# Moving TensorE transposes to DMA from tile 6 on, with two load buffers, later scores and split last rows, in a local attention + squared-ReLU kernel

## Chip, cores, metric

One core of one Trainium2 chip. The time is the device time of one execution in microseconds (us), the median of several. The page and the views of the profile are from one profiled execution each. A profiled span is about 1.8 us shorter than the time of the same run (before: span 220.5, time 222.32).

## The reference

```python
# attention: B, H, S, D = 4, 8, 768, 64; 8 global keys, 96 local ones
scores = q @ k.T / sqrt(D) + bias            # bias = -slope(head) * distance
scores = where(keep, scores, -1e9)           # keep: global or within the 96 before
a = softmax(scores);  x = a @ v              # x: 3072 tokens x 512
# two layers: w_in 512 x 2048, w_out 2048 x 512
h = x @ w_in;  r = maximum(h, 0);  out = (r * r) @ w_out
```

## The kernel before

The tokens are 24 tiles of 128 (six to a batch), and two tiles make a block of the two layers. For each tile: load q, k, v (cast to bf16 on the way, issued by GpSimd), transpose q and k, scores `sc`, exp on ScalarE, bias, `po` = weights @ v, normalise to `x`, transpose x. For each block, in eight steps: `hT` (first layer, 8 matmuls of 256 columns), relu on ScalarE, square on VectorE, `acc` (second layer, two pairs of 512 columns). A small planner in Python fixes each engine's order at build time, from guessed durations. TensorE runs that order strictly, so one operand that is late holds up all that stands behind it.

```python
NFIRST = 4; NBIAS = 3
JQK, JX = 10, 10            # from this tile on, q/k and x are transposed by DMA
NQ, NKT = 10, 2 * TPB       # load buffers for q and k
LEADS = {}                  # scores stand 12 steps before the block needs them
qk_ring = [const([P, 2, d_model], BF16, f"qk_{i}") for i in range(NQ)]
...
# below JQK: four transposes on TensorE into PSUM, one eviction; for q and for k
nc.tensor.transpose(out=tr[:, pair, :], in_=src[:, pair * P:(pair + 1) * P], identity=ident)
any_copy(e, T_[:, n], tr)
# from JQK on: one DMA for both, issued by SyncE
nc.sync.dma_start_transpose(out=T_.rearrange("p n a c -> p (n a) c"),
                            in_=qk_ring[j % NQ].rearrange("p n c -> p (n c)"))
...
# scores; for the first three tiles a second matmul adds the bias
nc.tensor.matmul(out=sc[odd, g][:, at, :], lhsT=..., rhs=..., start=True, stop=j >= NBIAS)
nc.tensor.matmul(out=sc[odd, g][:, at, :], lhsT=sid[2 * pair + odd], rhs=pb, start=False, stop=True)
...
# last block: first 128 rows over all steps, then the other 128 (whole width);
# the last rows leave PSUM as two halves of one bank: ScalarE, then VectorE; two stores
```

The softmax here doesn't subtract the row's maximum and nothing guards it: scores larger than these inputs give would overflow.

Of the kernel before, what the change touches and what calls it, by code (L numbers as in the profile page):

```python
# [11 lines left out]
FP32 = mybir.dt.float32  # L12
BF16 = mybir.dt.bfloat16
# [8 lines left out]
class Plan:  # L22
# [6 lines left out]



    LAG = {"PE": 0.25, "ACT": 0.15, "DVE": 0.12, "SP": 2.6, "POOLQ": 2.5, "DMA": 0.0}
    URGE = 0.05

    def __init__(self):
# [64 lines left out]
def kernel(  # L100
# [11 lines left out]
    nc = tc.nc  # L112
    B, H, S, D = q.shape
    P = 128
# [20 lines left out]
    NFIRST = 4  # L135
    NSPLIT = 4
    NBIAS = 3
    JQK, JX = 10, 10
    NQ, NKT = 10, 2 * TPB
    NG = 8 - NACC  # L140
    G = ("g", NG)

# [6 lines left out]
    def const(shape, dt, name):  # L149
        return consts.tile(shape, dt, name=name, tag=name)  # L150

    qk_ring = [const([P, 2, d_model], BF16, f"qk_{i}") for i in range(NQ)]
    v_sb = [const([P, H, D + 1], BF16, f"v_{j}") for j in range(NT)]

    qkT = [const([P, 2, NPAIR, P], BF16, f"qkT_{i}") for i in range(NKT)]
# [12 lines left out]
    pbt = const([P, 2, P], FP32, "pbt")  # L168
    pbw = const([P, 2, P], FP32, "pbw")
    plan = Plan()  # L170
    LEADS = {}
    NHS = 14
    E_AT = 14.0
    NWARM = 8
# [6 lines left out]
    def landed(name, at):  # L181
        land[name] = plan.op(("land",) + name, {"DMA": 0.0}, None, ready=at)

    def src_rows(x, j):
        b, t = divmod(j, TPB)
        return x[b, :, t * P : (t + 1) * P, :]

    def swdge(name, dst, src, t):
        nc.gpsimd.dma_start(out=dst, in_=src)  # L189
        issue[1] = max(issue[1], issue[0] + 3.3) + t  # L190
        issue[0] += 0.75 if name[0][0] == "w" else 0.88
        land[name] = issue[1] + 0.3

    plain = {}
    for j in range(NPLAIN):
# [12 lines left out]

    def load_part(n, j):
        swdge(  # L210
            ("qk"[n], j), qk_ring[j % NQ][:, n, :].rearrange("p (h d) -> p h d", h=H),
            src_rows((q, k)[n], j).rearrange("h p d -> p h d"), 0.85,
        )

# [117 lines left out]

    tiles = {}
    kT_users = [[] for _ in range(NKT)]
    qk_users = [[] for _ in range(NQ)]
    xT_op = {}
    xT_of = {}
    last_T = [None]
# [2 lines left out]
    for j in range(NT):  # L341
# [6 lines left out]
        if j in late:  # L348
            def emit_load(e, j=j):
                load_tile(j)  # L350
            ld = plan.op(
                ("load", j), {"POOLQ": 2.6}, emit_load, deps=qk_users[j % NQ] + [ones[j]],
                key=base, ready=issue[0],
            )
            qk_users[j % NQ] = []
            land["q", j] = land["k", j] = land["v", j] = ld


# [4 lines left out]
        for n in range(2) if j < JQK else ():  # L363
            users = []

            def emit_tr(e, j=j, n=n, fp=fp):
                tr = ps_g.tile([P, NPAIR, P], FP32 if fp else BF16, name="tr", tag="g")
                src = plain[n, j] if fp else qk_ring[j % NQ][:, n, :]
                for pair in range(NPAIR):
                    nc.tensor.transpose(  # L370
                        out=tr[:, pair, :], in_=src[:, pair * P : (pair + 1) * P],
                        identity=ident32 if fp else ident,
                    )
                tiles["tr", n, j] = tr

            tr = plan.op(
                ("tr", n, j), {"PE": 0.5 if fp else 0.24}, emit_tr,
                deps=[land["qk"[n], j]], key=base, takes=(*G, [users]),
            )

            def emit_T(e, j=j, n=n, T_=T_):
                any_copy(e, T_[:, n], tiles.pop(("tr", n, j)))

            c = plan.op(
                ("T", n, j), {"DVE": 0.7 if fp else 0.43, "ACT": 0.57}, emit_T,
                deps=[tr] + ku, key=base + 0.1,
            )
            users += [tr, c]
            parts.append(c)
            if not fp:  # L390
                qk_users[j % NQ].append(tr)
        if j >= JQK:
            def emit_dT(e, j=j, T_=T_):
                nc.sync.dma_start_transpose(
                    out=T_.rearrange("p n a c -> p (n a) c"),
                    in_=qk_ring[j % NQ].rearrange("p n c -> p (n c)"),
                )

            T = plan.op(
                ("T", j), {"SP": 2.0}, emit_dT,  # L400
                deps=[land["q", j], land["k", j], xT_op[j - 3]] + ku, key=base - 6,
            )
            qk_users[j % NQ].append(T)
            parts = [T]
        kT_users[j % NKT] = ku = []

# [6 lines left out]
        def emit_sc(e, gs, j=j, first=first):  # L413
# [8 lines left out]
                for kt in range(1 if first else 2)  # L422
            ]
            todo = [x for x in todo if x[0] in gs]
            for g, pair, at, kt in todo:
                for odd in range(2):
                    half = slice(odd * D, (odd + 1) * D)
                    nc.tensor.matmul(  # L428
                        out=sc[odd, g][:, at, :],
                        lhsT=qkT[(j - kt) % NKT][half, 1, pair, :],  # L430
                        rhs=qkT[j % NKT][half, 0, pair, :],
                        start=True,
                        stop=j >= NBIAS,
                        skip_group_check=True,
                    )
            for g, pair, at, kt in todo if j < NBIAS else ():
                for odd in range(2):
                    nc.tensor.matmul(
                        out=sc[odd, g][:, at, :],
                        lhsT=sid[2 * pair + odd],  # L440
                        rhs=pb0 if first else pb[:, kt, :],
                        start=False,
                        stop=True,
                        skip_group_check=True,
                    )
# [253 lines left out]

    for blk in range(NBLK):  # L700
        last = blk == NBLK - 1
        acc_users = [[], []]
        order2 = (
            [(s, sub) for sub in range(2) for s in range(NSTEP)]
            if last
            else [(s, sub) for s in range(NSTEP) for sub in range(2)]
        )
        for s, sub in order2:
            users = acc_users[sub]

            def emit_s2(e, blk=blk, s=s, sub=sub):
                if s == 0:
                    tiles["acc", blk, sub] = ps_acc.tile([P, d_model], FP32, name="acc", tag="acc")
                hs = tiles["hs", blk, s]
                for c in range(2):
                    nc.tensor.matmul(  # L716
                        out=tiles["acc", blk, sub],
                        lhsT=hs[:, c, sub * P : (sub + 1) * P],
                        rhs=w_out_sb[s][:, c, :],
                        start=(s == 0 and c == 0),  # L720
                        stop=(s == NSTEP - 1 and c == 1),
                        skip_group_check=True,
# [1 line left out]

            d, husers = square[blk, s]
            o = plan.op(
                ("s2", blk, s, sub), {"PE": 0.43}, emit_s2,
                deps=[d, land["wout", s]] + users[-1:],
                key=8 * blk + s + 2.0 + (50 if last and sub else 0),
                takes=("acc", NACC, [users]) if s == 0 else None,  # L730
            )
            users.append(o)
            husers.append(o)
            if s == NSTEP - 1:

                for half in (0, 1) if last and sub == 1 else (None,):
                    cols = (
                        slice(None)
                        if half is None
                        else slice(half * d_model // 2, (half + 1) * d_model // 2)  # L740
                    )
                    ousers = []

                    def emit_o(e, blk=blk, sub=sub, half=half, cols=cols):
                        o_sb = work.tile([P, d_model], FP32, name="o", tag="o", bufs=4)
                        any_copy(e, o_sb[:, cols], tiles["acc", blk, sub][:, cols])
                        tiles["o", blk, sub, half] = o_sb

                    costs = {"ACT": 0.57, "DVE": 0.62}
                    if half is not None:  # L750
                        costs = [{"ACT": 0.4}, {"DVE": 0.35}][half]
                    ev = plan.op(
                        ("o", blk, sub), costs, emit_o, deps=[o], key=8 * blk + s + 1.0,
                        takes=("o", 4, [ousers]),
                    )
                    users.append(ev)
                    ousers.append(ev)

                    def emit_st(e, blk=blk, sub=sub, half=half, cols=cols):
                        r0 = (blk * 2 + sub) * P  # L760
                        nc.sync.dma_start(
                            out=out[r0 : r0 + P, cols],
                            in_=tiles.pop(("o", blk, sub, half))[:, cols],
                        )

                    st = plan.op(
                        ("st", blk, sub), {"SP": 0.4}, emit_st, deps=[ev],
                        key=8 * blk + s + 9.0,
                    )
                    ousers.append(st)  # L770

    for o in plan.run({"PE": 4.2, "DVE": 4.4, "ACT": 4.2}):
        if o["emit"]:
            o["emit"](o["engine"])

# [34 lines left out]
```

## Time and profile before

221.8 us (221.15 to 222.0, 3 runs). The table is made from the busy times of each engine in stretches of the profiled run (us). "Idle" is the length less TensorE's busy time.

| stretch | length | TensorE idle | what it is |
|---|---|---|---|
| 0 to 12 | 12 | 3.5 | start-up |
| 12 to 30 | 18 | 2.7 | all DMA engines full, weights and first tiles arrive; granted clock 0.50 from 14.1 to 17.5 |
| 30 to 60 | 30 | 1.4 | 1.1 of it is one wait of tile 6 |
| 60 to 200 | 140 | 1.3 | TensorE full: the view of waits has no row here, and 32 of the 2024 matmuls have no record in this trace (1992 records, 2024 of weight loads), so much of the 1.3 need not be idle |
| 200 to 220.5 | 20.5 | 4.7 | last block, 4.1 after the last matmul |

How to read the views: PE is TensorE, PEld its weight loads, DVE VectorE, ACT ScalarE, POOL GpSimd, SP SyncE (SPq: its DMA issues). Rows of digits on a page are the span in 40 equal slices: busy tenths of PE and of the 16 DMA engines (9 is 90% or more), and as PEclk the TensorE clock that was granted, in tenths of full speed. Waits are "who waited <- for whom: us in total, times, longest". The chain by time is "start, us, what". A timeline row is "start, us, engine, line, operation, out<-in, count [idle before <- releaser]". Line numbers shift with the change: scores L428 -> L435, q/k transposes L370 -> L376, first layer L652 -> L661, second layer L716 -> L731, DMA transposes of q and k L394 -> L400, of x L628 -> L637, stores L761 -> L766.

### The profile page before, as it was taken

The numbers are of one execution on the slowest core, as the hardware profiler recorded it, in microseconds if no ns is written. First come the engines' busy times: TensorE is split into PE (matmuls) and PEld (weight loads), VectorE is DVE, ScalarE is ACT, GpSimd is POOL, SyncE is SP. The second block draws the span as 40 slices with busy tenths as digits, with TensorE's granted clock in tenths as the row PEclk, the third lists the DMA queues.
The fourth block names the chain that finished last, engine by engine and source line by source line (L and its number), as shares of the span: only waits on it lengthen the run. The fifth ranks groups of instructions, "written<-read, shape, count | busy, mean of one in ns | idle before, by whom it ended". The sixth has DMA issues, their size and how long they took to land.

```text
span 220.5 us, 5058 instructions
## 1 busy us (share of the span) xinstructions
PE 206.9 (94%) x1992; PEld 143.5 (65%) x2024; DVE 144.0 (65%) x372; ACT 122.5 (56%) x224; POOL 73.7 (33%) x91
## 2 busy tenths in 40 slices
PE   7779879799999999999999999999999999999992
PEld 3658658457667676676667667666667766766740
DVE  5456858647677786775668668666767768745520
ACT  3648865626846657545636736733845744724430
POOL 7997658797962996404000000000000000000000
PEclk9979999999999999999999999999999999999998
DMA  9999999999999999999542532531730620310211
GB/s 129 148 167 200 180 190 192 165 208 161 165 189 131 155 199 145 158 197 132 140 60 48 144 54 45 147 64 33 168 72 4 166 27 12 109 24 16 82 38 59
DMA packets 107304, 26.03 MB, mean 118 GB/s; under 512 B 97936, under 2 KB 104336, under 8 KB 107280
## 3 DMA queue, kind: packets, MB, share of 16 engines
q0 software_dynamic: 79200, 13.37, 82.3%
q1 hardware_dynamic: 28080, 12.33, 25.7%
q8 instruction: 16, 0.26, 0.5%
q14 instruction: 8, 0.07, 0.1%
HBM read 27.26 MB, written 6.29 MB: 152 GB/s over the span
## 4 chain that ended last, share of the span: by engine, by line
PE 77%; DMA 12%; POOL 6%; issue 2%; DVE 1%; ACT 0%; POOLq 0%
PE hT L652 34%; PE acc L716 34%; DMA wout<-in_moe_w_out_dram 4%; PE sc L428 4%; DMA win<-in_moe_w_in_dram 4%; PE po L541 4%; DMA qk<-in_q_dram 4%; POOL qk L189 2%; POOL v L189 2%; POOL win L189 1%; PE tr L370 1%; POOL wout L189 1%; PE trx L604 1%; DVE hs L685 0%; ACT hr L673 0%
## 5 line engine op out<-in xcount | busy, mean ns | idle before, releaser
L652 PE MATMUL hT<-xT,win 128*128 128x256 bf16 x768 | 99.0, 273 | 0.2
L716 PE MATMUL acc<-wout,hs 128*128 128x512 bf16 x352 | 91.5, 379 | 2.0 <-DVE hs L685 0.6
L673 ACT ACTIVATE hr<-hT 128x512 f32<-128x512 f32 x96 | 57.3, 597 | 55.6 <-PE hT L652 54.1
L652 PEld LDWEIGHTS <-win 128*128 128x128 bf16 x768 | 71.1, 98 | 16.7
L685 DVE TENSOR_TENSOR hs<-hr 128x512 bf16<-128x512 f32 x96 | 65.0, 689 | 23.3 <-ACT hr L673 22.5
L716 PEld LDWEIGHTS <-hs 128*128 128x128 bf16 x384 | 36.6, 98 | 29.1 <-DVE hs L685 1.2
L474 ACT ACTIVATE esc<-sc 128x512 bf16<-128x512 f32 x78 | 42.3, 599 | 14.7 <-PE sc L428 14.7
L499 DVE TENSOR_TENSOR at<-esc,E 128x512 bf16<-128x512 bf16 x78 | 32.7, 421 | 8.6 <-ACT esc L474 7.2
L189 POOL DMA_DIRECT2D qk<-in_q_dram x23 | 20.8, 904 | 14.8 <-DMA qkT<-qk 9.0
L189 POOL DMA_DIRECT2D v<-in_v_dram x24 | 21.5, 896 | 7.6 <-DVE at L499 2.7
L189 POOL DMA_DIRECT2D qk<-in_k_dram x23 | 20.6, 897 | 2.8 <-DMA v<-in_v_dram 2.1
L569 DVE TENSOR_TENSOR x<-po,rs 128x256 bf16<-128x256 f32 x48 | 20.4, 424 | 1.7
L541 PEld LDWEIGHTS <-at 128*128 128x128 bf16 x352 | 16.7, 98 | 4.8
L541 PE MATMUL po<-v,at 128*128 128x65 bf16 x352 | 18.5, 193 | 0.0
L428 PEld LDWEIGHTS <-qkT 64*128 64x128 bf16 x352 | 10.0, 95 | 10.9 <-issue 8.0
L568 DVE RECIPROCAL rs<-po 128x4 f32<-128x4 f32 x48 | 8.5, 178 | 10.9 <-PE po L541 10.8
L428 PE MATMUL sc<-qkT 64*128 64x128 bf16 x192 | 13.4, 221 | 1.7 <-ACT qkT L300 0.9
L300 ACT COPY o<-acc 128x512 f32<-128x512 f32 (+1 forms) x15 | 8.4, 573 | 9.2 <-PE acc L716 8.3
L302 DVE COPY o<-acc 128x512 f32<-128x512 f32 (+1 forms) x10 | 6.6, 664 | 9.6 <-PE acc L716 5.0
L428 PE MATMUL sc<-qkT,qkT 64*128 64x128 bf16 x160 | 11.6, 218 | 0.0
L370 PE MATMUL tr<-ident,qk 128*128 128x128 bf16 x72 | 6.8, 225 | 4.0 <-DMA qk<-in_q_dram 2.1
L370 PEld LDWEIGHTS <-qk 128*128 128x128 bf16 x72 | 4.9, 101 | 6.1 <-DMA qk<-in_q_dram 3.0
(40 smaller groups left out, 72.9 us busy)
## 6 DMA issues: line engine op xcount, KB each, us to landing
out_dram<-o SPq DMA_DIRECT2D x23, 256.0 KB, 2.7
v<-in_v_dram POOLq DMA_DIRECT2D x24, 128.0 KB, 7.6
qk<-in_q_dram POOLq DMA_DIRECT2D x23, 128.0 KB, 7.4
qk<-in_k_dram POOLq DMA_DIRECT2D x23, 128.0 KB, 7.7
win<-in_moe_w_in_dram POOLq DMA_DIRECT2D x8, 256.0 KB, 8.1
wout<-in_moe_w_out_dram POOLq DMA_DIRECT2D x8, 256.0 KB, 8.8
plain<-in_q_dram SPq DMA_DIRECT2D x1, 256.0 KB, 3.2
plain<-in_k_dram SPq DMA_DIRECT2D x1, 256.0 KB, 3.9
```

The lines of the kernel that those rows point to most:

```text
L189: nc.gpsimd.dma_start(out=dst, in_=src)
L370: nc.tensor.transpose(out=tr[:, pair, :], in_=src[:, pair * P : (pair + 1) * P], identity=ident32 if fp else ident,)
L428: nc.tensor.matmul(out=sc[odd, g][:, at, :], lhsT=qkT[(j - kt) % NKT][half, 1, pair, :], rhs=qkT[j % NKT][half, 0, pair, :], start=True, s ...
L474: nc.scalar.activation(out=esc, in_=tiles.pop(("sc", j, odd, g)).rearrange("p a c -> p (a c)"), func=Act.Exp, scale=scale,)
L499: nc.vector.tensor_mul(at, tiles.pop(("esc", j, odd, g)), bias)
L541: nc.tensor.matmul(out=po[:, hi, :], lhsT=tiles["at", j, odd, g][:, at * P : (at + 1) * P], rhs=v_sb[kj][:, h, :], start=(i == 0), stop=(i ...
L568: nc.vector.reciprocal(rs, po[:, :, D : D + 1])
L569: nc.vector.tensor_tensor(out=x[:, 4 * hf : 4 * hf + 4, :], in0=po[:, :, :D], in1=rs.to_broadcast([P, 4, D]), op=Alu.mult,)
L652: nc.tensor.matmul(out=hT[:, c, :], lhsT=w_in_sb[s][:, kt, c * P : (c + 1) * P], rhs=tiles["xT", blk][:, kt, :], start=(kt == 0), stop=(kt ...
L673: nc.scalar.activation(hr, tiles.pop(("hT", blk, s)), Act.Relu)
L685: nc.vector.tensor_mul(hs, hr, hr)
L716: nc.tensor.matmul(out=tiles["acc", blk, sub], lhsT=hs[:, c, sub * P : (sub + 1) * P], rhs=w_out_sb[s][:, c, :], start=(s == 0 and c == 0) ...
```

## The change

The intent: take tiles 6 to 9 off TensorE, which bounds the kernel; give those DMA transposes time (scores of tiles 6 and 7 two steps later); replace ten load buffers by six single-use ones and a ring of two; correct the planner's guesses of when data land; split the last 128 rows of the output into column halves, each with its own sum; and set the start flag only on the first score matmul in a PSUM bank, so that the bias adds on to the scores.

```diff
-    LAG = {... "SP": 2.6, "POOLQ": 2.5, "DMA": 0.0}
+    LAG = {... "SP": 2.6, "POOLQ": 0.8, "DMAQ": 1.2, "DMA": 0.0}
-    JQK, JX = 10, 10
-    NQ, NKT = 10, 2 * TPB
+    JQK, JX = 6, 6
+    NQ, NKT = 2, 2 * TPB
-    qk_ring = [... for i in range(NQ)]
+    qk_ring = [... for i in range(NFIRST + 2 + NQ)]
-    LEADS = {}
+    LEADS = {6: 10, 7: 10}
+    def slot(j):
+        return j if j < NFIRST + 2 else NFIRST + 2 + j % NQ
-        land[name] = issue[1] + 0.3
+        land[name] = issue[1] + 0.3 + min(max(0.1 * (issue[1] - 8), 0.0), 1.6)
+            ld = plan.op(("data", j), {"DMAQ": 2.7}, None, deps=[ld], key=base)
 (scores)
-                        start=True,
+                        start=j >= NBIAS or (odd, g) not in opened,
 (last block)
+        parts = [(0, None), (1, 0), (1, 1)] if last else [(0, None), (1, None)]
+            own = half == 1                  # second half: a bank of the other pool
-                        rhs=w_out_sb[s][:, c, :],
+                        rhs=w_out_sb[s][:, c, cols],
-                        costs = [{"ACT": 0.4}, {"DVE": 0.35}][half]
+                    {"ACT": 0.57, "DVE": 0.62} if half is None else {"ACT": 0.37},
 (the rest: index qk_ring by slot(j), and bookkeeping of the planner)
```

More of the change, by code (lines that the diff above doesn't have):

```diff
@@ L22 @@
 class Plan:
-    LAG = {"PE": 0.25, "ACT": 0.15, "DVE": 0.12, "SP": 2.6, "POOLQ": 2.5, "DMA": 0.0}
+    LAG = {"PE": 0.25, "ACT": 0.15, "DVE": 0.12, "SP": 2.6, "POOLQ": 0.8, "DMAQ": 1.2, "DMA": 0.0}
     URGE = 0.05
@@ L150, in const @@
         return consts.tile(shape, dt, name=name, tag=name)
-    qk_ring = [const([P, 2, d_model], BF16, f"qk_{i}") for i in range(NQ)]
+    qk_ring = [const([P, 2, d_model], BF16, f"qk_{i}") for i in range(NFIRST + 2 + NQ)]
     v_sb = [const([P, H, D + 1], BF16, f"v_{j}") for j in range(NT)]
@@ L210, in load_part @@
         swdge(
-            ("qk"[n], j), qk_ring[j % NQ][:, n, :].rearrange("p (h d) -> p h d", h=H),
+            ("qk"[n], j), qk_ring[slot(j)][:, n, :].rearrange("p (h d) -> p h d", h=H),
             src_rows((q, k)[n], j).rearrange("h p d -> p h d"), 0.85,
@@ L334 @@
     kT_users = [[] for _ in range(NKT)]
-    qk_users = [[] for _ in range(NQ)]
+    qk_users = [[] for _ in qk_ring]
     xT_op = {}
@@ L351 @@
             ld = plan.op(
-                ("load", j), {"POOLQ": 2.6}, emit_load, deps=qk_users[j % NQ] + [ones[j]],
+                ("load", j), {"POOLQ": 2.6}, emit_load, deps=qk_users[slot(j)] + [ones[j]],
                 key=base, ready=issue[0],
             )
-            qk_users[j % NQ] = []
+            qk_users[slot(j)] = []
+            ld = plan.op(("data", j), {"DMAQ": 2.7}, None, deps=[ld], key=base)
             land["q", j] = land["k", j] = land["v", j] = ld
@@ L367, in emit_tr @@
                 tr = ps_g.tile([P, NPAIR, P], FP32 if fp else BF16, name="tr", tag="g")
-                src = plain[n, j] if fp else qk_ring[j % NQ][:, n, :]
+                src = plain[n, j] if fp else qk_ring[slot(j)][:, n, :]
                 for pair in range(NPAIR):
@@ L390 @@
             if not fp:
-                qk_users[j % NQ].append(tr)
+                qk_users[slot(j)].append(tr)
         if j >= JQK:
@@ L395, in emit_dT @@
                     out=T_.rearrange("p n a c -> p (n a) c"),
-                    in_=qk_ring[j % NQ].rearrange("p n c -> p (n c)"),
+                    in_=qk_ring[slot(j)].rearrange("p n c -> p (n c)"),
                 )
@@ L402 @@
             )
-            qk_users[j % NQ].append(T)
+            qk_users[slot(j)].append(T)
             parts = [T]
@@ L424, in emit_sc @@
             todo = [x for x in todo if x[0] in gs]
+            opened = set()
             for g, pair, at, kt in todo:
@@ L435, in emit_sc @@
                     )
+                    opened.add((odd, g))
             for g, pair, at, kt in todo if j < NBIAS else ():
@@ L701, with emit_s2 @@
         last = blk == NBLK - 1
-        acc_users = [[], []]
+        acc_users = {}
+        parts = [(0, None), (1, 0), (1, 1)] if last else [(0, None), (1, None)]
         order2 = (
-            [(s, sub) for sub in range(2) for s in range(NSTEP)]
+            [(s, *p) for p in parts for s in range(NSTEP)]
             if last
-            else [(s, sub) for s in range(NSTEP) for sub in range(2)]
+            else [(s, *p) for s in range(NSTEP) for p in parts]
         )
-        for s, sub in order2:
-            users = acc_users[sub]
-            def emit_s2(e, blk=blk, s=s, sub=sub):
+        for s, sub, half in order2:
+            users = acc_users.setdefault((sub, half), [])
+            w = d_model if half is None else d_model // 2
+            cols = slice(0, w) if half is None else slice(half * w, (half + 1) * w)
+            own = half == 1
+            def emit_s2(e, blk=blk, s=s, sub=sub, half=half, w=w, cols=cols, own=own):
                 if s == 0:
-                    tiles["acc", blk, sub] = ps_acc.tile([P, d_model], FP32, name="acc", tag="acc")
+                    pool, tag = (ps_g, "g") if own else (ps_acc, "acc")
+                    tiles["acc", blk, sub, half] = pool.tile([P, w], FP32, name="acc", tag=tag)
                 hs = tiles["hs", blk, s]
@@ L716, in emit_s2 @@
                     nc.tensor.matmul(
-                        out=tiles["acc", blk, sub],
+                        out=tiles["acc", blk, sub, half],
                         lhsT=hs[:, c, sub * P : (sub + 1) * P],
-                        rhs=w_out_sb[s][:, c, :],
+                        rhs=w_out_sb[s][:, c, cols],
                         start=(s == 0 and c == 0),
@@ L726 @@
             o = plan.op(
-                ("s2", blk, s, sub), {"PE": 0.43}, emit_s2,
+                ("s2", blk, s, sub), {"PE": 0.43 * w / d_model}, emit_s2,
                 deps=[d, land["wout", s]] + users[-1:],
-                key=8 * blk + s + 2.0 + (50 if last and sub else 0),
-                takes=("acc", NACC, [users]) if s == 0 else None,
+                key=8 * blk + s + 2.0 + (0 if not last else 8 * sub + 8 * (half or 0)),
+                takes=((*G, [users]) if own else ("acc", NACC, [users])) if s == 0 else None,
             )
@@ L734 @@
             if s == NSTEP - 1:
-                for half in (0, 1) if last and sub == 1 else (None,):
-                    cols = (
-                        slice(None)
-                        if half is None
-                        else slice(half * d_model // 2, (half + 1) * d_model // 2)
-                    )
-                    ousers = []
-                    def emit_o(e, blk=blk, sub=sub, half=half, cols=cols):
-                        o_sb = work.tile([P, d_model], FP32, name="o", tag="o", bufs=4)
-                        any_copy(e, o_sb[:, cols], tiles["acc", blk, sub][:, cols])
-                        tiles["o", blk, sub, half] = o_sb
-                    costs = {"ACT": 0.57, "DVE": 0.62}
-                    if half is not None:
-                        costs = [{"ACT": 0.4}, {"DVE": 0.35}][half]
-                    ev = plan.op(
-                        ("o", blk, sub), costs, emit_o, deps=[o], key=8 * blk + s + 1.0,
-                        takes=("o", 4, [ousers]),
-                    )
-                    users.append(ev)
-                    ousers.append(ev)
-                    def emit_st(e, blk=blk, sub=sub, half=half, cols=cols):
-                        r0 = (blk * 2 + sub) * P
-                        nc.sync.dma_start(
-                            out=out[r0 : r0 + P, cols],
-                            in_=tiles.pop(("o", blk, sub, half))[:, cols],
-                        )
-                    st = plan.op(
-                        ("st", blk, sub), {"SP": 0.4}, emit_st, deps=[ev],
-                        key=8 * blk + s + 9.0,
-                    )
-                    ousers.append(st)
@@ L772, with emit_o @@
-    for o in plan.run({"PE": 4.2, "DVE": 4.4, "ACT": 4.2}):
+                ousers = []
+                def emit_o(e, blk=blk, sub=sub, half=half, cols=cols):
+                    o_sb = work.tile([P, d_model], FP32, name="o", tag="o", bufs=4)
+                    any_copy(e, o_sb[:, cols], tiles["acc", blk, sub, half])
+                    tiles["o", blk, sub, half] = o_sb
+                ev = plan.op(
+                    ("o", blk, sub), {"ACT": 0.57, "DVE": 0.62} if half is None else {"ACT": 0.37},
+                    emit_o, deps=[o], key=8 * blk + s + 1.0, takes=("o", 4, [ousers]),
+                )
@@ new lines, with emit_st @@
+                users.append(ev)
+                ousers.append(ev)
+                def emit_st(e, blk=blk, sub=sub, half=half, cols=cols):
+                    r0 = (blk * 2 + sub) * P
+                    nc.sync.dma_start(
+                        out=out[r0 : r0 + P, cols],
+                        in_=tiles.pop(("o", blk, sub, half))[:, cols],
+                    )
+                st = plan.op(
+                    ("st", blk, sub), {"SP": 0.4}, emit_st, deps=[ev],
+                    key=8 * blk + s + 9.0,
+                )
@@ L773 @@
+                ousers.append(st)
+    for o in plan.run({"PE": 4.2, "DVE": 4.4, "ACT": 4.2, "DMAQ": issue[1]}):
         if o["emit"]:
```

## The prediction

> **What bounds the kernel now.** I read the page first, then the table of stretches, TensorE's waits, the chain of waits by time, and last the timeline of the tail.
>
> ```profile
> PE 206.9 (94%) x1992; PEld 143.5 (65%) x2024; DVE 144.0 (65%) x372; ACT 122.5 (56%) x224; POOL 73.7 (33%) x91
> PE   7779879799999999999999999999999999999992
> PEclk9979999999999999999999999999999999999998
> DMA  9999999999999999999542532531730620310211
> ```
>
> TensorE (PE) is full from the tenth slice on (one slice is 5.5 us), so there its work sets the time. Before about 43 us it has holes, and DMA is saturated. The fourth slice also has a lower granted clock.
>
> ```profile
> PE tr L370 <- DMA qk<-in_q_dram: 2.1, 2, 1.1
> PE tr L370 <- DMA qk<-in_k_dram: 1.9, 2, 1.4
> PE sc L428 <- ACT qkT L300: 0.9, 2, 0.5
> ...
> 15.16 8.84 DMA win<-in_moe_w_in_dram
> 24.29 9.82 DMA wout<-in_moe_w_out_dram
> 34.40 8.29 DMA qk<-in_q_dram
> 42.73 0.40 PE tr L370 x4
> ```
>
> The first three are TensorE's waits (total, times, longest): it waits for q and k of a tile because the transpose of that tile stands next in its order. The other four are from the chain: up to 42.7 us the end is set by a row of loads, after that by TensorE alone, until the tail:
>
> ```profile
> 211.00 0.61 ACT hr L673
> 211.63 0.70 DVE hs L685
> 212.38 4.07 PE acc L716 x18
> ...
> 216.47 0.37 ACT L300 COPY o<-acc 128x256 f32<-128x256 f32 x1 [2.87 <-PE acc L716]
> 216.88 0.42 DVE L302 COPY o<-acc 128x256 f32<-128x256 f32 x1 [4.56 <-ACT o L300]
> 217.33 0.81 SPq L761 DMA_DIRECT2D out_dram<-o  x2
> ```
>
> The last relu and square (211.00 to 212.33) are followed by 18 matmuls, then by a ScalarE copy and a VectorE copy one after the other. The last store leaves after 217.3, and the span ends at 220.5.
>
> **What the Trainium skill says.** (1) "TensorE: Matmul & The Clock Gate", section "Wait — 56ns, not 53.3ns?": warm matmuls start every 55.6 ns at 128 columns and 215.7 ns at 512. The trace agrees: in the chain eight transposes take 0.45 us (56 ns each) and four 512-column matmuls 0.86 us (215 ns). The 219 and 379 ns of the groups contain pipeline depth and are not the cost. (2) "DMA: Bandwidth & Descriptors", "Queues, rings and completion order": every DMA engine takes packets in turn from the queues that have work, so a transpose issued by SyncE shares the engines with GpSimd's loads. The trace agrees: a DMA transpose of q and k lands in 3.2 us when it is issued at 99 us, but in 10.2 us (median of two) at 58 to 62 us, beside loads. (3) "PSUM — Partial Sum Buffer", "The four PSUM rules": a matmul that starts a group clears the written bits of its whole bank, and a later one that doesn't start overwrites where the bit is clear. So the bias of the first three tiles overwrites most scores in the kernel before. The new flag repairs values; it adds no instruction. No time in the trace bears on it. (4) Same page, "PSUM bank collisions raise a hardware error": two engines may not touch one bank at once. The trace shows the order that results: VectorE's last copy starts 0.04 us after ScalarE's ends.
>
> **The change part by part.** I compared the build's order of instructions: TensorE has 64 rows fewer.
>
> *Transposes of tiles 6 to 9 go to DMA.* Removed: 4 tiles x (8 of q and k + 4 of x) = 48 TensorE matmuls; 48 x 56 ns = 2.7 us. They stood at 42 to 83 us, where TensorE is 97 to 99% busy, so I count all of it. 12 evictions of 0.42 us (VectorE) or 0.59 us (ScalarE) go too, but both engines are idle for a third and more: worth nothing. Added: eight DMA transposes, on the queue of SyncE, which is free.
>
> *Waits.* Tile 6's transpose on TensorE waited 1.1 us for q (41.6 to 42.7 us), with work of the second layer standing behind it. In the new order that work comes first: between the last w_out use of block 0 and the scores of tile 6 stand 10 pairs of 512-column matmuls (4.3 us), two groups of eight 256-column ones (1.75), 16 of po (0.5) and one transpose of x (0.2), 6.8 us in all. At tile 4 the score matmuls waited 0.45 us for a copy; the new order puts a first-layer group between transpose and scores. So 1.1 + 0.45 = 1.55 us may go. The 1.4 us wait for k of tile 4 stays: the load order up to tile 6 is the same.
>
> *What the DMA path gives back.* k of tile 6 is issued at 35.3 and lands after 8.3, at 43.6 us. The new transpose starts then. Outstanding beside it are v of tile 6 and q, k, v of tile 7 (landing till 47), but nothing more, as tile 8's load waits for this transpose's buffer. I estimate 5 to 6 us, between the 3.2 of a free DMA and the 10.2 of a full one: it lands at 49 to 50. TensorE reaches the scores of tile 6 at: last w_out lands 33.1 + 8.7 = 41.8; two pairs with it end at 42.7; plus 6.8 us: 49.5. So I take off 0.4 us for a wait there. Tile 7 has 8 us more and waits for nothing.
>
> *Two buffers.* Loads of tile 8 and later start when the transpose two tiles earlier has landed. Round trip: 2.6 us of issue, some 5 us to land, 3.3 to 6 us of transpose: 11 to 14 us, against two tiles of TensorE work, 2 x 8.1 us (scores at 83.39 and 91.48). It fits with 2 us at least, and the initial backlog gives more. Worth nothing, except that loads no longer crowd the queue.
>
> *Last rows in halves.* 16 matmuls of 512 columns become 32 of 256: 16 x 216 = 3.46 us against 32 x 109 (0.87 us per eight) = 3.49: nothing. But four pairs of halves (0.87 us) now stand between the first layer's end and the last product that needs the last square. Before, two pairs (0.86 us) stood against the 1.38 us from 211.00 to 212.38: the 0.5 us of idle goes. After the last matmul one ScalarE copy of 0.37 us is left and not the 0.42 us of VectorE behind it; with the shorter store queue 0.45 us.
>
> *Bias.* 0.
>
> Sum: 2.7 + 1.55 - 0.4 + 0.5 + 0.45 = 4.8 us; 221.8 - 4.8 = 217.0.
>
> **The rivals.** *A. The wait moves:* the DMA transposes are slow among loads and TensorE waits for tile 6, or for x of tile 7, which has about 3.7 us from its normalisation to its first use. For it: the 10.2 us at 58 us, and 7.1 us for one of x at 89.75 us. Against it: then eight loads were under way, now four and falling. At 10 us tile 6 lands at 54 and TensorE stands for 4 us: gain 1.2, time 220.6. *B. TensorE gains only its own work:* the start is set by loads, whose order is unchanged, so idle removed at 42 us comes back as waits for w_out at 39 to 42 us. For it: win and wout are in the chain with 8.8 and 9.8 us. Then 2.7 + 0.95 - 0.4 = 3.2: 218.6. *C. More than the sum:* fewer competing loads at 45 to 100 us and a better filled start also end the low-clock slice at 11 to 16 us, worth up to 1.7 us (granted 0.72 over 6 us): 215.3. Against it: nothing in that stretch changes but the place of some transposes.
>
> **Range and chances.** The centre is the sum, 217.0. A and B pull up, C down: 215.0 to 219.7. 2% faster is 217.36, hardly above the centre; A and B together I give 0.42, a slowdown (A with several tiles, over 9 us of new waiting) 0.01. Faster 0.57, same 0.42, slower 0.01.
>
> **What would show it.** In the changed profile: PE busy near 203 to 204 us of a span near 215.7; no wait of transposes for q at 42 us; scores of tile 6 at about 49.5 with a wait under 1 us; DMA transposes of tile 6 landing in 5 to 6 us; no wait of the first layer for x; DMA's row below 9 in the slices from the ninth; one ScalarE copy of 256 columns alone after the last matmul. It is wrong if scores wait for DMA transposes by more than 2 us in all, if waits for win or wout appear, or if the low-clock slice is gone or longer.

## The result, and the profile after

The changed kernel takes **215.69 us** (215.55 to 216.55, 4 runs), the kernel before 221.9 in the same rounds. The ratio is 0.9735, with a 95% interval of 0.9701 to 0.9769: faster by 2.6%. A ratio here is the mean time of one kernel's fast runs over that of the other's of the same rounds, so it isn't quite the ratio of the medians.

The page of the changed kernel, the rows that answer to those of before:

```profile
PE 206.2 (96%) x1992; PEld 141.8 (66%) x1992; DVE 141.9 (66%) x366; ACT 118.7 (55%) x218; POOL 74.1 (35%) x91
PE   7889899999999999999999999999999999999994
PEclk9999999999999999999999999999999999999999
DMA  9999999999999999999969969999989910310202
```

TensorE is full from the sixth slice on (before: the ninth). Don't read busy time as the gain: it fell by 0.7 us only, while the span fell by 6.6. Busy spans overlap, and a record that is missing makes it smaller: before's trace lacks 32 matmuls, and the changed kernel itself shows 206.2 here and 204.7 in e5, whose trace lacks 32 too. The DMA row is solid up to the twentieth slice and nearly so up to the thirty-second, where before it fell after the nineteenth: the same loads are spread out. The DMA engines didn't become free, but less was under way at once: the time of all packets in 48 to 60 us is 2.33 times the span of the 16 engines before, and 1.44 times after.

TensorE's waits over the whole run, the three on DMA:

```profile
PE acc L731 <- DMA wout<-in_moe_w_out_dram: 0.7, 1, 0.7
PE tr L376 <- DMA qk<-in_k_dram: 0.4, 1, 0.4
PE hT L661 <- DMA win<-in_moe_w_in_dram: 0.3, 1, 0.3
```

Before, 4.0 us of waits of TensorE transposes for q and k stood here. From 30 us to the end the same view has no row at all. The chain by time shows TensorE alone from 29.6 us on, where before loads held it until 42.7:

```profile
20.40 9.17 DMA win<-in_moe_w_in_dram
...
29.62 1.92 PE hT L661 x16
...
42.79 2.62 PE acc L731 x12
...
49.10 0.33 PE sc L435 x8
...
205.97 4.80 PE acc L731 x38
...
210.80 0.37 ACT o L305
```

The row at 42.79 is the work that stood behind tile 6's transpose before. The two last rows are the tail: 38 matmuls without a gap, and one copy. SyncE's last three stores (before, it was issuing until 218.14):

```profile
208.79 2.74 SPq L766 DMA_DIRECT2D out_dram<-o  x3
```

The first DMA transpose (tile 6): SyncE's timeline, and the issues in the window of 43 to 44 us (count, us to landing):

```profile
43.04 1.38 SPq L400 DMA_TRANSPOSE qkT<-qk  x1
```

```profile
qkT<-qk SPq DMA_TRANSPOSE x1, 5.0
```

It lands at 48.04, and TensorE reaches its scores at 49.04: no wait.

**Where the 6.6 us of span come from**, by four marks in the two traces (one profiled run each, us):

| from ... to | before | after | gain |
|---|---|---|---|
| start ... scores of tile 6 | 49.18 | 49.04 | 0.14 |
| ... scores of tile 23 | 138.41 | 133.56 | 4.85 |
| ... end of the last matmul | 28.85 | 28.17 | 0.68 |
| ... end of the span | 4.06 | 3.13 | 0.93 |

The first two rows belong together. Up to tile 6's scores, the changed order holds 2.1 us more work on balance, 2.6 more of the two layers and 0.45 less of tile 6's transposes (39.5 against 37.4 us, counted from the orders at the start-to-start times of matmuls in the chain: 56 ns at 128 columns, 109 at 256, 216 at 512). So 4.85 + 0.14 = 5.0 us is 2.7 us of transposes that TensorE no longer does, and 2.3 us that TensorE no longer loses before tile 6. Before's stretch of low clock explains little of the 2.3: e2 below has before's order without that stretch in its profile, and starts these scores at 48.92, 0.26 us earlier.

### The profile page after: what moved, and what is told of

Its sections match the earlier page's. It is cut to its first block, busy times and chain, and to the rows that moved or that the text cites. A ratio compares the mean times of both kernels' runs of the same rounds, so it can differ in the third digit from the quotient of the medians.

```text
span 213.9 us, 5031 instructions
## 1 busy us (share of the span) xinstructions
PE 206.2 (96%) x1992; PEld 141.8 (66%) x1992; DVE 141.9 (66%) x366; ACT 118.7 (55%) x218; POOL 74.1 (35%) x91
## 4 chain that ended last, share of the span: by engine, by line
PE 86%; DMA 7%; POOL 4%; issue 1%; DVE 0%; ACT 0%; POOLq 0%
PE hT L661 38%; PE acc L731 38%; PE sc L435 5%; PE po L550 5%; DMA win<-in_moe_w_in_dram 4%; DMA qk<-in_k_dram 3%; POOL qk L193 2%; POOL v L193 2%; POOL win L193 1%; PE tr L376 0%; PE trx L613 0%; DVE x L578 0%; ACT o L305 0%; POOL pbi L244 0%; DVE v L595 0%
## 5 line engine op out<-in xcount | busy, mean ns | idle before, releaser
L731 PE MATMUL acc<-wout,hs 128*128 128x512 bf16 (+1 forms) x400 | 95.6, 370 | 0.7 <-DMA wout<-in_moe_w_out_dram 0.7
L731 PEld LDWEIGHTS <-hs 128*128 128x128 bf16 x400 | 38.4, 98 | 28.5 <-issue 0.8
L577 DVE RECIPROCAL rs<-po 128x4 f32<-128x4 f32 x48 | 8.6, 179 | 10.2 <-PE po L550 10.2
L305 ACT COPY o<-acc 128x512 f32<-128x512 f32 (+1 forms) x14 | 7.8, 557 | 9.2 <-PE acc L731 9.2
L307 DVE COPY o<-acc 128x512 f32<-128x512 f32 x11 | 7.6, 691 | 6.1 <-PE acc L731 6.1
L524 DVE COPY qkT<-qkT 128x32 bf16<-128x32 bf16 x16 | 3.8, 235 | 7.4 <-PE sc L435 7.3
L193 POOL DMA_DIRECT2D win<-in_moe_w_in_dram x8 | 6.7, 840 | 0.6 <-DMA wout<-in_moe_w_out_dram 0.6
```

Source lines behind the costliest of these rows:

```text
L193: nc.gpsimd.dma_start(out=dst, in_=src)
L305: nc.scalar.copy(dst, src)
L577: nc.vector.reciprocal(rs, po[:, :, D : D + 1])
L731: nc.tensor.matmul(out=tiles["acc", blk, sub, half], lhsT=hs[:, c, sub * P : (sub + 1) * P], rhs=w_out_sb[s][:, c, cols], start=(s == 0 an ...
```

## The experiments

Each kernel ran in five rounds against the kernel before on the same chip, in four calls, each on another chip: the first four, the next four, the next three, and the last. Medians are of fast runs; e1, e5 and e8 also had one slow run each (221.93, 219.69, 220.1), e12 four. Each pair of marks is from one profiled run. "After" is the changed kernel. The last column but one is the start of tile 6's and tile 23's scores in the profiled run.

| run | median us of fast runs | ratio to before, 95% | scores of 6, 23 | span |
|---|---|---|---|---|
| before | 221.9 | 1 | 49.18, 187.59 | 220.5 |
| after | 215.69 | 0.9735 (0.9701-0.9769) | 49.04, 182.60 | 213.9 |
| e1 old tail | 217.94 | 0.9834 (0.9803-0.9866) | 51.06, 184.65 | 217.5 |
| e2 new tail alone | 220.26 | 0.9917 (0.9899-0.9935) | 48.92, 187.32 | 218.6 |
| e3 transposes back | 218.70 | 0.9849 (0.9829-0.9869) | 50.72, 185.65 | 216.9 |
| e4 old guesses | 217.81 | 0.9803 (0.9768-0.9838) | 49.36, 185.17 | 216.5 |
| e5 after, again | 215.92 | 0.9751 (0.9718-0.9784) | 48.98, 182.55 | 213.8 |
| e6 DMA transposes alone | 225.31 | 1.0156 (1.0137-1.0175) | 51.03, 190.17 | 223.1 |
| e7 six buffers | 224.53 | 1.0112 (1.0075-1.0149) | 51.88, 192.00 | 223.3 |
| e8 old flag | 217.46 | 0.9778 (0.9742-0.9815) | 48.74, 184.14 | 215.4 |
| e9 tile 7 earlier | 216.66 | 0.9762 (0.9738-0.9787) | 49.29, 184.01 | 215.3 |
| e10 no later scores | 216.00 | 0.9732 (0.9704-0.9760) | 48.96, 183.40 | 214.7 |
| e11 x of 6, 7 on TensorE | 216.82 | 0.9775 (0.9747-0.9803) | 49.35, 183.36 | 214.8 |
| e12 from tile 5 | 220.71 | 0.9932 (0.9906-0.9958) | profile slow | - |

All results were correct by the comparison with the reference.

### e1 and e2: the tail

e1 is the changed kernel with the block loop of before; e2 is the kernel before with the block loop of after (the "last block" part of the diff).

> The changed kernel with the last block as it was before (whole last rows, evicted by ScalarE and then VectorE). My theory, from the two traces: the last rows in halves are worth 0.5 us of idle before the last products and 0.9 us after the last matmul, so this runs at 215.7 + 1.4 = 217.1 us. Rival (the prediction's own size, 0.5 + 0.45): 216.65. Rival that the tail gains nothing and the whole gain is from the start and the transposes: 215.7. In the trace a ScalarE and a VectorE copy of 256 columns stand one after the other at the end, and the span after the last matmul is 4.0 us and not 3.1.

> The kernel before with nothing but the last rows in halves. My theory: the same 1.4 us come off here, 221.9 - 1.4 = 220.5 us. If the tail's gain leans on the rest of the change, it is less than 1 us (over 220.9).

The tail of e1, from the chain by time:

```profile
208.06 0.61 ACT hr L682
...
208.69 0.70 DVE hs L694
...
209.44 4.07 PE acc L725 x18
...
213.54 0.38 ACT o L305
...
213.94 0.42 DVE o L307
```

This is before's tail again. The timed e1 is 2.2 us slower than after, more than 1.4 and more than any rival; but its profiled run (219.31, one of the two slowest of the five fast ones) is already 2.02 us late at tile 6, in a part where its TensorE order is the same as after's (the orders agree row by row up to the last block): it waited 2.0 us for a win load, and then the granted clock was 0.50 from 26.3 to 29.7 us. From the scores of tile 23 to the end of the span, where the edit lies, e1 takes 217.5 - 184.65 = 32.85 us and after 213.9 - 182.60 = 31.30: the tail is worth **1.55 us**. e2 says the same from the other side: before 32.91, e2 31.28, so 1.63, and timed 0.8% (1.8 us, interval 1.4 to 2.2). My 1.4 was near, and the prediction's own size (0.95) was too small. The late start of e1 was left open, and is why e5 was run.

### e3: transposes back on TensorE

```diff
-    JQK, JX = 6, 6
+    JQK, JX = 10, 10
```

> The changed kernel with the transposes of tiles 6 to 9 back on TensorE, all else left (two buffers, later scores, new order). My theory: 48 matmuls of 56 ns come back on a full TensorE, 2.7 us: 218.4 us, and no new wait, since the transpose of tile 6 now has other work before it. Rival: the transposes were only an obstacle in the order, their 2.7 us lie in holes that are there anyway: under 217. Other rival: with them the wait for q of tile 6 comes back: 219.5 or more.

218.70 us (218.62 to 218.77) where 218.4 was expected. Tile 23's scores come 3.05 us later than in after, for 2.67 us of work put back. TensorE's waits in e3 have none beyond 30 us, so the wait for q of tile 6 doesn't return although its transpose is on TensorE again: q lands at 42.43 us (before: 42.68), and the transpose now stands at 47.58. What removed that wait is the new order, not DMA. And e3, with no new DMA transpose at all, is already 3.3 us faster than before: 1.6 of it is the tail, and the 1.7 that are left I put down to the order. The trace agrees: up to tile 6's scores e3 has 3.4 us more work than before, and starts them only 1.5 us later. Which of the planner's guesses, the later scores and the buffers makes that order no run separates.

### e4: the planner's old guesses

```diff
-    LAG = {... "POOLQ": 0.8, "DMAQ": 1.2, "DMA": 0.0}
+    LAG = {... "POOLQ": 2.5, "DMA": 0.0}
-        land[name] = issue[1] + 0.3 + min(max(0.1 * (issue[1] - 8), 0.0), 1.6)
+        land[name] = issue[1] + 0.3
-            ld = plan.op(("data", j), {"DMAQ": 2.7}, None, deps=[ld], key=base)
```

> The changed kernel with the planner's old guesses of when loads land, which gives TensorE the old order up to tile 5 (tile 4's scores before the second block's first group) and the new one from tile 6. My theory: the better order in the first 30 us is worth about 1 us of the gain (the waits of 1.0 us at tile 2 and 1.4 us at tile 4 are gone in the changed kernel, 1.0 us of waits for win and wout came in their place, and the low-clock stretch went): 216.7 to 217.2 us, with the low granted clock back at 12 to 18 us. Rival: loads set the start, whatever the order: 215.7, the same as the changed kernel.

217.81 us, but for another reason than mine. Tile 6's scores start at 49.36, only 0.3 us later than in after, and the granted clock is not low. The loss is a wait that after doesn't have:

```profile
PE hT L660 <- DMA xT<-x: 2.1, 1, 2.1
```

So my theory (1 us from the order in the first 30 us) fell. What the better order is worth there can't be told from this: e1, with the new order, was 2 us late. In this one profile it is little: e4 has before's order up to tile 5, after's work up to tile 6's scores, and is 0.3 us late there; so most of the 2.3 us lies in what stands between tile 5 and tile 6.

### e5: the change again; e8: the old start flag

e5 has no edit. e8:

```diff
-                        start=j >= NBIAS or (odd, g) not in opened,
+                        start=True,
```

> The changed kernel once more, unedited, to see its own spread. Why: the kernel with the old tail (the run before) has the same TensorE order up to the last block, yet its profiled run reached the scores of tile 6 at 51.06 us against 49.04, with one 2.0 us wait for a win load. If that is chance in the loads of the first 30 us, the changed kernel's own runs here spread as widely (over 1 us between fast runs) around 215.7 to 216.5, and its profile may show such a wait too. If they stay within 0.3 us of 215.7, the old tail costs the start something that I don't see.

> The changed kernel with the old start flag on every score matmul of the first three tiles. No theory gives it time: the same as the changed kernel's repeat within 0.3%. It tells whether the flag can be left out of the explanation.

e5: fast runs of 215.35, 215.87, 215.92, 216.49 and 217.87 us, and one slow one of 219.69. The spread is over 2 us within fast runs, so e1's late start is no outlier; e5's own profile shows no such wait. e8 has the same spread: 215.24 to 218.07, and the interval of its ratio overlaps that of e5. No time of the flag is shown, but the runs don't tell 0.3% apart as I wanted: each ratio is known to about 0.35%, their difference to about 0.5% (1 us). The profile is sharper: the flag acts on tiles 0 to 2, and e8 starts tile 6's scores at 48.74, no later than after or e5. e8's profile caught the wait of e4 again; its chain by time:

```profile
60.11 3.96 DMA qk<-in_k_dram
...
64.17 5.73 DMA xT<-x
...
69.94 1.05 PE hT L661 x8
```

The first layer of block 3 waited 1.7 us for x of tile 7. Compare SyncE's timeline in e8 (first fence) and in after (second):

```profile
64.17 1.21 SPq L637 DMA_TRANSPOSE xT<-x  x1
65.48 1.44 SPq L400 DMA_TRANSPOSE qkT<-qk  x1
```

```profile
64.46 1.19 SPq L637 DMA_TRANSPOSE xT<-x  x1
66.27 1.23 SPq L400 DMA_TRANSPOSE qkT<-qk  x1
```

In after, k of tile 10 landed late, the transpose of tile 10 left 1.8 us after that of x, and x took 3.6 us. In e8 it left 1.3 us after, and x took 5.7 (in e4: 1.3 and 6.1). e5's profile has 1.4 and 3.3, though, and no wait. So the nearness of the next transpose goes along with the slow ones, but alone it doesn't decide.

### e6 and e7: loads that run on

e6 is the kernel before with one line: `JQK, JX = 6, 6`, its ten buffers left. e7 is the changed kernel with more buffers:

```diff
-    NQ, NKT = 2, 2 * TPB
+    NQ, NKT = 6, 2 * TPB
```

> The kernel before with the transposes of tiles 6 to 9 on DMA and nothing else: ten load buffers, so loads run on, and the old places of the scores. My theory (two buffers matter because they clear the queue): the transpose of tile 6 starts at 43.6 us beside eight loads and lands in some 10 us, at 53 to 54; TensorE is there at about 48, and waits 5 us; more for later tiles. 221.9 - 2.7 - 1.2 + 5.5 = 223.5 us. Rival (the transpose takes 5 us anyway, buffers are worth nothing, as the prediction said): wait under 1 us, 218.5 us.

> The changed kernel with six buffers in place of two beside the first six, so that the loads of tiles 8 to 11 run on behind tile 7's. TensorE's order is the same. My theory: the transpose of tile 6 takes 8 to 10 us and not the 5.0 us of the changed kernel, landing at 51 to 53; TensorE waits 2 to 4 us at the scores of tile 6: 218 to 220 us. Rival: no change, 215.7.

The part of the change that carries its name makes the kernel **slower** by itself: 225.31 us. And e7, which differs from after in nothing but four more load buffers, takes 224.53, over 8 us more than after. In e6, the issue of tile 6's transpose (us to landing), TensorE's wait for it, and the stretch with the end of that wait (the first figures are its length and TensorE's busy time, 2.97 of 6 us; the third from the end is the granted clock, 0.77 on average):

```profile
qkT<-qk SPq DMA_TRANSPOSE x1, 8.1
```

```profile
PE sc L428 <- DMA qkT<-qk: 4.5, 1, 4.5
```

```profile
48.00:54.00 6.00, 2.97 (x19) 1.77 (x20) 0.88 (x3) 1.68 (x3) 2.94 (x4) 0.77 2.05 156
```

TensorE's waits of e7 from 45 to 100 us, and three of its stretches:

```profile
PE hT L661 <- DMA xT<-x: 3.2, 1, 3.2
PE sc L435 <- DMA qkT<-qk: 2.5, 1, 2.5
```

```profile
48.00:54.00 6.00, 3.46 (x24) 1.70 (x22) 2.24 (x4) 1.92 (x4) 2.63 (x3) 0.85 1.66 145
52.20:55.60 3.40, 3.40 (x16) 1.80 (x13) 0.85 (x2) 1.09 (x2) 0.00 (x0) 0.50 1.79 129
76.10:79.50 3.40, 3.06 (x11) 1.61 (x12) 0.53 (x1) 0.60 (x1) 0.00 (x0) 0.50 1.75 155
```

In e7 the transpose of tile 6 took 8.6 us to land (5.0 in after), 2.5 us of wait followed, and then the granted clock was half for 3.4 us; after the second wait (3.2 us) again. In 3.4 us at half clock TensorE does the work of 1.7, so each such stretch costs about 1.7 us (an estimate from these two rows). The waits (5.7 us) and the two stretches (3.4 us) make 9.1 of the 9.4 us by which tile 23's scores are later than in after. e6 has the same from 51.25 to 54.65 us, after its wait of 4.5. Both results were worse than I expected (223.5; 218 to 220), because I had counted the waits only. The mechanism holds: few load buffers keep the queue short, and with it short the transposes were faster (5.0 us against 8.6 for tile 6, 4.1 against 11.5 for tile 7).

### e9, e10, e11: the wait for x of tile 7

```diff
-    LEADS = {6: 10, 7: 10}
+    LEADS = {6: 10}                 (e9)      LEADS = {}   (e10)
-    JQK, JX = 6, 6
+    JQK, JX = 6, 8                  (e11)
```

> The changed kernel with only tile 6's scores two steps later; tile 7's at their old place. Why: the changed kernel's runs spread from 215.35 to 217.87 us, and two profiles of nearly the same program show a wait of 1.7 and 2.1 us of the fourth block's first layer for x of tile 7 by DMA, which the changed kernel's own two profiles don't have. My theory: that wait is the spread, it comes when the q and k transpose of tile 10 leaves right behind it (6 us to land and not 3.5), and two steps more of slack remove it: fast runs within 1 us, 215.7 or a little less, no wait for x. The transpose of tile 7 lands at 49.6 us, its scores are reached at 53, so no wait there. Rival: the spread is from the loads of the first 30 us; then the median stays at 216.2 and the spread as it was.

> The changed kernel with neither tile's scores later. Tells what 'two steps later' is worth. TensorE reaches tile 6's scores 0.8 us of work earlier, at 48.2, and its transpose lands at 48.0: a wait of 0 to 0.5 us, and no wait for x of tile 7. My theory: 215.5 to 216.2 us, as good as the change, so the later scores are worth nothing. Rival (the later scores are needed): waits at tiles 6 and 7, 217 us or more.

> The changed kernel with the x of tiles 6 and 7 transposed on TensorE, all else left. 8 matmuls of 56 ns come back, 0.45 us. My theory: the spread goes with the wait for x, 216.1 us at the least spread; the changed kernel's mean of fast runs (216.3) is not beaten by more than 0.3. Rival (spread from the first loads): 216.7 with the same spread.

e9: fast runs within 0.6 us (four of them), as I said, but around 216.66, and its profile has a wait of 1.0 us for x: issued 3 us earlier, it fell into the loads of the next tile and took 7.5 us. The miss: an earlier start isn't more slack when it moves a transfer into a crowd. e10: 216.0, ratio 0.9732, the same as after within the intervals: putting the scores two steps later is worth nothing that these runs can show. e11: no wait for x by DMA, 216.82, at or a little above what its 0.45 us of matmuls explains. None beats the change. The spread stays in e10 (215.28 to 217.03), whose profile (216.5) has no wait for x but a granted clock of 0.72 in 12 to 18 us, and reaches tile 6's scores at 48.96 with 0.8 us less work before them than after; so the start has a part in it too, and how much each has stays open.

### e12: from tile 5

```diff
-    JQK, JX = 6, 6
+    JQK, JX = 5, 5
```

> The changed kernel with tile 5 on DMA transposes too (12 TensorE matmuls less, 0.67 us). Tests the rule that a DMA transpose pays only when the load queue behind it is short: k of tile 5 lands at about 35 us, with the last weights and tiles 6 and 7 still queued behind it. My theory: its transpose takes 8 to 10 us, landing at 43 to 45, and TensorE, which reaches the scores of tile 5 at about 41 (31.8 us of work + 9.3 us lost so far), waits 2 to 4 us: 217.5 to 220 us. Rival (a transpose costs 5 us wherever it stands): it lands at 40, no wait, 215.3 to 215.7 us.

220.71 us (fast runs 219.61 to 222.71), a little worse than the 217.5 to 220 expected. Four of nine runs were slow, 225.25 to 226.59, at a mean granted clock of 0.977 to 0.982; over all nine the median is 222.71. As e7's low clock came after waits, the fast runs alone may show the edit's cost too small. The profiled run was a slow one, so only its transfer is used, not its time: the transpose of tile 5 was issued at 34.96 and took

```profile
qkT<-qk SPq DMA_TRANSPOSE x1, 9.2
```

to land, at 44.2, inside the 43 to 45 that I gave. With the last weights and two tiles in the queue a DMA transpose costs 9 us and not 5. Tile 6 is the first whose transpose has nothing but v of its own tile and one more tile behind it; of the starts tried, 5, 6 and 10 (e3), it is the best.

## Why the prediction was right

The time (215.69 in 215.0 to 219.7) and the direction (faster by over 2%) were right; 217.0 was 1.3 us too high. Term by term:

- **Transposes, 2.7 us: held.** e3 puts them back and loses 3.0 us of median time (2.8 against e5), 3.05 in the trace.
- **Waits, 1.55 us, less 0.4 for tile 6: too small.** What TensorE lost before tile 6 fell by 2.3 us in the trace, by 1.7 in e3's times. The 1.1 us wait for q is gone as said, and through the order as said (e3). The 0.4 us of wait for the DMA transpose didn't come: it landed at 48.04 (said: 49 to 50), in 5.0 us (said: 5 to 6). The 1.4 us wait for k of tile 4, which I said would stay, isn't in after's profile; but such waits come and go from run to run of one program (e1, e5), so that part is no gain that I can claim.
- **Tail, 0.5 + 0.45 us: mis-sized.** It measured 1.55 and 1.63 us. The gap before the last products gave 0.68 up to the last matmul. After it 0.93 and not 0.45 came off: I counted VectorE's 0.42 us and took the shorter store queue for almost nothing. But before, both last stores left only after VectorE's copy, 0.81 us of issue for two. After, one of them left long before: SyncE's issue ends 0.76 us after the last matmul (211.53), before 1.70 (218.14).
- **Two buffers, "worth nothing, except that loads no longer crowd the queue": the exception was the point.** The round trip did fit, as worked out. But without the short queue the change loses: e7 is over 8 us slower than after. The number was in my text (rival A, 10.2 us), though not as the value of that part.
- **Bias, 0: held** (e8, to about 0.5%, and in its profile up to tile 6). That the flag repairs values was argued from the skill; no run here compares the errors, and e2 and e8, which have the old flag, passed the comparison with the reference too.
- **Rivals.** A came in its second form and partly: x of tile 7 had "about 3.7 us" by my count, and some runs miss it by 1.7 to 2.1 us (e4, e8). B (idle comes back as waits for weights) showed as 1.0 us at 23 to 26 us, and at 39 to 42 not at all. C named the low-clock slice as worth up to 1.7 us: it was gone, but that isn't a gain. In e1's rounds five runs of the kernel before with a mean granted clock of 0.998 to 1.0 have a mean of 221.91 us, and the four with 0.988 to 0.992 one of 222.09. Nor is it the change that ends it: e2, in before's order, has no such slice in its profile, and e10, in nearly the changed order, has one.
- **Its own signs.** "What would show it" missed twice: PE busy is 206.2 us of 213.9 and not 203 to 204, and DMA's row is not below 9 from the ninth slice on but at 9 up to the twentieth, since the loads were spread and not removed. Of its three signs of being wrong two came: waits for win and wout (0.3 and 0.7 us), and the low-clock slice gone. By the runs neither undoes the sum: these waits are far smaller than the 4.0 us that went, and the low clock comes and goes in one program. It also counted two slices wrong: on its page PE is full from the ninth, not the tenth, and the low clock is in the third, not the fourth.

The three gains at the end: tail 1.6 us (e1 and e2, each by itself), transposes 3.0 (e3 against after), and the order 1.7. The last is what is left of 6.2 us, so that they add up proves nothing; the trace's 2.3 us (1.9 in e3) is the only other measure of it.

## What to carry to other kernels

A transpose taken off a full engine and given to DMA is worth its time only if it lands before it is needed, and that is set by how many loads are queued beside it: limit the loads that may run ahead (few buffers) before moving it, and start at the first tile behind which the queue is short. Count a wait of TensorE as more than its length: here stretches of half clock followed several of them (e1, e6, e7). On an engine that runs in a fixed order, put work that is ready in front of work whose data is about to land; the wait then goes whoever does the transpose. At the end of a kernel, count the store issues after the last product as well as the copies.

## What the Trainium skill lacked or had wrong

- "DMA: Bandwidth & Descriptors": says that queues are served in turn, but not what that does to the latency of a DMA transpose. Here one of q and k (128 x 1024 elements, bf16) landed in 3.2 us on a quiet DMA, 5.0 beside four loads (tile 6 of after), and 8.1 to 11.7 beside a queue kept full (the first three of e6 and of e7).
- Same page, "Rules for kernel authors": of a transpose beside ordinary DMAs it says that it "needs nothing". That holds for correctness only: with loads left to run on, these transposes made the kernel 1.1 to 1.6% slower than before (e6, e7).
- "TensorE: Matmul & The Clock Gate", "Why this matters for your kernels": it warns of TensorE idle for over about 3 us. Here shorter ones were also followed by half the clock for 3.4 us: waits of 2.5 us (e7, 2.54 us idle in 48 to 54) and 2.0 us (e1). One of 2.1 us was not (e4).
- No page that I read says that more load buffers can make a kernel slower: six in place of two cost over 8 us here (e7 against after).
